# A long convolution split at half the sequence, and its kernel generated on one array tile per channel

## The chip, the cores and the metric

The program runs on one core of one Trainium2 chip. The metric is the device time of one execution in microseconds (us), median of several executions. A profile adds a span, which is the time from the first to the last instruction; it is about 1.9 us shorter than the timed execution. Engines are called PE (TensorE, the matrix engine), PEld (its weight loads, which overlap PE: in before the two are busy for 92% and 50% of the span), DVE (VectorE), ACT (ScalarE), POOL (GpSimd) and SP (SyncE, which issues most loads and stores). "N=256" is a matmul with 256 columns of moving data.

Every kernel below was timed alternately with the kernel before, on the same chip.

## The reference, cut to what matters

```python
def reference(u, A_re, A_im, B_re, B_im, C_re, C_im, log_dt, Dskip, x, w_gate, w_up, w_down):
    # L = 2048 positions, D = 512 channels, N = 128 modes per channel, F = 1792; x is u
    xn = layernorm(u)
    K  = einsum("dn,dnl,dn->dl", C, exp(dt * A * l), dt * B).real   # one kernel of 2048 taps per channel
    y  = irfft(rfft(pad(xn)) * rfft(pad(K)))[:L] + xn * Dskip       # causal convolution along the sequence
    g  = (sigmoid(xn @ w_gate) * (xn @ w_up)) @ w_down              # a gated linear unit (GLU)
    return u + y + g
```

The convolution and the GLU depend on `xn` alone, so they run interleaved: the GLU's matmuls fill TensorE while VectorE prepares the convolution.

## The kernel before

The convolution works in the frequency domain, with spectra of 4,096 points in 32 groups. The channels are in two column halves of 256 (`p`), and each half has 8 units (`u`) of four groups, so there are 16 units. The parts that matter:

```python
# 1. kernel generation: VectorE builds tables G and H for 128 channels, TensorE multiplies them.
#    Four channel blocks c, two halves each. G is one buffer: block c+1 seeds it after block c's matmuls.
for half_ in range(2):
    def f_k(...):
        for y in range(16 * half_, 16 * half_ + 16):
            R, h = 4 * (y % 4) + y // 8, y // 4 % 2
            pk = ...                                   # PSUM
            for comp in range(2):
                for t in range(2):                     # two column tiles of 64, two channels in each
                    r = slice(4 * R + 2 * t, 4 * R + 2 * t + 2)
                    T.matmul(pk[64 * t:64 * t + 64, y % 8, :], G[:, r, :, comp, h], H[:, r, :, comp, h],
                             start=(comp == 0), stop=(comp == 1), tile_position=(0, 64 * t))
# ...
# 2. one unit
def fm(...):  ...            # forward matmuls, 8 x N=256; evicted by ScalarE into xx, halves swapped by DMA
def fk(...):                 # spectrum of K: 20 matmuls of N=256 into a pair of PSUM banks
    for r in range(GB):      # GB = 4 groups
        for kt in range(NKT):          # NKT = 5
            T.matmul(two(sk)[:, DW * r:DW * r + DW], es()[:, r, kt, :], kT[p][:, kt, :], ...)
# ScalarE evicts it to kb, of which there is ONE slot
def fp(...):                 # the product of the spectra: one multiply of 128x2048 on VectorE
    V.tensor_tensor(out=pp()..., in0=xx()..., in1=kb().unsqueeze(1).to_broadcast([128, 2, GB * DW]), op=ALU.mult)
def fv(...):  ...            # product matmuls, 16 x N=256, into a PSUM pair; evicted, stored
```

A list `ORDER` fixes the order of all operations, so each engine has a fixed sequence. The change does not touch that list.

## Time and profile before

Time: 268.42 us median (267.21 to 268.91, 4 runs); the profiled execution, with a span of 262.9 us, is not one of these four, whose spans would be 265.3 to 267.0 us.

From about 20 to 145 us VectorE's row has only nines, and it is the first entry of the chain. From about 171 us on VectorE has holes, and TensorE carries the chain.

The groups of instructions of the parts that change (line, engine, operation, output and input, shape, count; then busy us and mean ns of one; then the engine's idle time before them and what ended it):

```profile
L817 DVE TENSOR_TENSOR big<-big 128x2048 bf16<-128x2048 bf16 x16 | 19.5, 1220 | 26.7 <-ACT big L813 15.6
L660 DVE TENSOR_TENSOR big<-big 128x256 bf16<-128x256 bf16 (+4 forms) x52 | 31.2, 600 | 2.8 <-ACT big L682 2.6
```

L817 is the product of the spectra, L660 the table work (its 2.6 us wait, at 149.9 us, is the one interruption of VectorE's chain; it waits for a block's tables to be released). TensorE's timeline gives the real cost of each group, from one start to the next (start, duration, operation, count; in brackets the idle time before it and what ended it):

```profile
82.50 2.12 PE L724 MATMUL pair_64<-big 128*64 128x42 bf16 x64
84.45 2.08 PE L724 MATMUL pair_63<-big 128*64 128x42 bf16 x64
...
145.15 0.63 PE L827 MATMUL pair_63<-big 64*64 64x256 bf16 x16 [0.70 <-ACT big L813]
...
158.70 2.35 PE L810 MATMUL pair_64<-big 128*128 128x256 bf16 x20
...
171.50 2.07 PE L724 MATMUL pair_63<-big 128*64 128x42 bf16 x62 [0.28 <-DVE big L666]
```

L724 is the kernel generation, L827 the product matmuls. A generation half takes 1.95 us (82.50 to 84.45), a K spectrum (L810) 2.18 us, and the last block's generation starts at 171.5 us. This last number is the yardstick: to its left VectorE sets the pace, to its right TensorE does.

### The profile page before, as it was taken

To read this page: it belongs to the slowest core of one execution; us is meant where nothing else is said; L and a number is where in the kernel's file an instruction comes from. 1 tells how busy PE (TensorE), PEld (TensorE's weight loads), DVE (VectorE), ACT (ScalarE), POOL (GpSimd) and SP (SyncE) were. 2 spreads that over 40 slices of the span, in tenths; PEclk is the share of its full clock that TensorE was granted. 3 is DMA by queue.
4 is the path that set the end of the run, shared out by engine and by line. 5 is a ranking of instruction groups with operands and counts; after the bars stand their busy time and mean duration, and the time that the engine had idled before them with its cause. 6 is when DMAs were issued, how large, how long until landed. Compare 5 with 4: busy or idle time off the path is not lost.

```text
span 262.9 us, 5705 instructions
## 1 busy us (share of the span) xinstructions
PE 243.0 (92%) x2254; PEld 131.4 (50%) x2254; DVE 192.9 (73%) x389; ACT 157.9 (60%) x247; POOL 21.7 (8%) x41
## 2 busy tenths in 40 slices
PE   7689998899999989989999999999999999999990
PEld 2353333334336444747567557477457656444440
DVE  3889999999999999999999599924111223566323
ACT  2699999999996544294674845752536776310000
POOL 1300220072000000102000000000020200000000
PEclk9999999999999999999999999999999999999997
DMA  7999975664559022857978846947997983496123
GB/s 163 161 295 323 339 220 145 190 139 107 145 202 157 15 80 80 228 178 143 306 216 253 228 118 193 271 124 235 302 306 175 308 261 96 131 264 201 44 67 100
DMA packets 50924, 49.34 MB, mean 188 GB/s; under 512 B 13137, under 2 KB 44114, under 8 KB 50770
## 3 DMA queue, kind: packets, MB, share of 16 engines
q1 hardware_dynamic: 47362, 44.66, 60.0%
q0 software_dynamic: 960, 1.57, 3.7%
q10 hardware_dynamic: 2576, 2.75, 3.6%
q8 instruction: 17, 0.28, 0.4%
q14 instruction: 9, 0.07, 0.1%
HBM read 30.36 MB, written 12.06 MB: 161 GB/s over the span
## 4 chain that ended last, share of the span: by engine, by line
DVE 47%; PE 28%; DMA 11%; SPq 4%; issue 3%; ACT 3%; DVEq 1%; POOL 1%; ACTq 0%
DVE big L661 8%; DVE big L660 8%; DVE hT_sb L928 8%; DVE big L665 5%; DVE big L666 5%; PE bank_68 L946 5%; SPq L382 4%; PE pair_64 L810 3%; DVE stats L482 3%; DMA big<-z_scr 3%; DMA big<-c_E 2%; DVE big L611 2%; PE bank_67 L921 2%; DMA big<-v_scr_94 2%; DVE big L609 2%
## 5 line engine op out<-in xcount | busy, mean ns | idle before, releaser
L946 PE MATMUL bank_68<-wd_sb,hT_sb 128*128 128x512 bf16 x196 | 44.7, 379 | 1.3 <-ACT glu_sb L976 1.1
L817 DVE TENSOR_TENSOR big<-big 128x2048 bf16<-128x2048 bf16 x16 | 19.5, 1220 | 26.7 <-ACT big L813 15.6
L906 PEld LDWEIGHTS <-wg_sb 128*128 128x128 bf16 x236 | 21.9, 97 | 29.1 <-issue 8.7
L921 PEld LDWEIGHTS <-wu_sb 128*128 128x128 bf16 x224 | 21.0, 97 | 28.8 <-issue 6.5
L946 PEld LDWEIGHTS <-hT_sb 128*128 128x128 bf16 x224 | 21.1, 98 | 27.6 <-issue 3.9
L810 PEld LDWEIGHTS <-big 128*128 128x128 bf16 x320 | 30.8, 98 | 6.7 <-DMA big<-c_E 1.4
L660 DVE TENSOR_TENSOR big<-big 128x256 bf16<-128x256 bf16 (+4 forms) x52 | 31.2, 600 | 2.8 <-ACT big L682 2.6
L661 DVE TENSOR_TENSOR big<-big 128x256 bf16<-128x256 bf16 (+4 forms) x52 | 31.3, 601 | 0.0
L921 PE MATMUL bank_67<-xnT,wu_sb 128*128 128x512 bf16 x88 | 22.6, 379 | 0.3 <-DVE hT_sb L928 0.2
L665 DVE TENSOR_TENSOR big<-big 128x128 bf16<-128x128 bf16 (+4 forms) x52 | 21.4, 412 | 0.6
L810 PE MATMUL pair_64<-big 128*128 128x256 bf16 x180 | 21.2, 273 | 0.6 <-DMA big<-c_E 0.6
L666 DVE TENSOR_TENSOR big<-big 128x128 bf16<-128x128 bf16 (+4 forms) x52 | 21.2, 407 | 0.0
L906 PE MATMUL bank_65<-xnT,wg_sb 128*128 128x512 bf16 (+1 forms) x80 | 19.7, 368 | 1.3 <-ACT hT_sb L915 0.9
L906 PE MATMUL bank_67<-xnT,wg_sb 128*128 128x512 bf16 (+1 forms) x76 | 18.5, 368 | 2.2 <-DVE hT_sb L928 2.2
L928 DVE TENSOR_TENSOR hT_sb<-hT_sb,bank_67 128x512 bf16<-128x512 bf16 x22 | 15.0, 682 | 7.4 <-PE bank_67 L921 7.3
L906 PE MATMUL bank_66<-xnT,wg_sb 128*128 128x512 bf16 (+1 forms) x80 | 19.7, 369 | 0.7 <-DVE hT_sb L928 0.4
L921 PE MATMUL bank_66<-xnT,wu_sb 128*128 128x512 bf16 x72 | 18.5, 380 | 0.2 <-ACT hT_sb L915 0.2
L921 PE MATMUL bank_65<-xnT,wu_sb 128*128 128x512 bf16 x64 | 16.4, 379 | 1.1 <-ACT hT_sb L915 0.5
L928 DVE TENSOR_TENSOR hT_sb<-hT_sb,bank_66 128x512 bf16<-128x512 bf16 x18 | 12.3, 681 | 6.7 <-PE bank_66 L921 3.8
L724 PEld LDWEIGHTS <-big 128*64 128x64 bf16 x512 | 16.1, 157 | 2.2 <-DVE big L666 1.0
L813 ACT ACTIVATE big<-pair_64 128x1024 bf16<-128x1024 f32 x9 | 9.2, 1023 | 13.3 <-PE pair_64 L810 11.1
L915 ACT ACTIVATE hT_sb<-bank_66 128x512 bf16<-128x512 f32 x19 | 11.7, 615 | 8.0 <-PE bank_66 L906 8.0
(117 smaller groups left out, 356.2 us busy)
## 6 DMA issues: line engine op xcount, KB each, us to landing
big<-c_E SPq DMA_DIRECT2D x16, 640.0 KB, 5.7
z_scr<-big SPq DMA_DIRECT2D x16, 256.0 KB, 2.8
big<-z_scr SPq DMA_DIRECT2D x16, 256.0 KB, 5.2
big<-big SPq DMA_DIRECT2D x64, 64.0 KB, 3.3
big<-in_A_u_dram SPq DMA_DIRECT2D x8, 256.0 KB, 7.5
v_scr_94<-big SPq DMA_DIRECT2D x8, 256.0 KB, 3.3
big<-v_scr_94 SPq DMA_DIRECT2D x8, 256.0 KB, 4.6
v_scr_95<-big SPq DMA_DIRECT2D x8, 256.0 KB, 4.0
```

The lines of the kernel that those rows point to most:

```text
L660: V.tensor_tensor(out=wide(outp), in0=lov, in1=mre, op=ALU.mult)
L661: V.tensor_tensor(out=wide(tb()), in0=lov, in1=mim, op=ALU.mult)
L665: V.tensor_tensor(out=outp[:, :, :, 0, :], in0=outp[:, :, :, 0, :], in1=tb()[:, :, :, 1, :], op=opr)
L666: V.tensor_tensor(out=outp[:, :, :, 1, :], in0=outp[:, :, :, 1, :], in1=tb()[:, :, :, 0, :], op=opi)
L724: T.matmul(pk[64 * t:64 * t + 64, y % 8, :], G[:, r, :, comp, h], H[:, r, :, comp, h], start=(comp == 0), stop=(comp == 1), tile_position= ...
L810: T.matmul(two(sk)[:, DW * r:DW * r + DW], es()[:, r, kt, :], kT[p][:, kt, :], start=kt == 0, stop=kt == NKT - 1)
L817: V.tensor_tensor(out=pp().rearrange("p c g d -> p c (g d)"), in0=xx().rearrange("p c g d -> p c (g d)"), in1=kb().unsqueeze(1).to_broadca ...
L906: T.matmul(bank(sl)[:, c0:c1], w[:, kt, k * 128:(k + 1) * 128], xnT[:, grp, kt, c0:c1], start=(kt == 0), stop=(kt == KT - 1))
L915: S.activation(out=hT_sb[:, hs.idx, k % 2, :], in_=bank(sl), func=ACT.Sigmoid)
L921: T.matmul(bank(sl), wu_sb[:, kt, k * 128:(k + 1) * 128], xnT[:, grp, kt, :], start=(kt == 0), stop=(kt == KT - 1))
L928: V.tensor_tensor(out=h(), in0=h(), in1=bank(sl), op=ALU.mult)
L946: T.matmul(bank(po), hT_sb[:, hts[k // 2].idx, k % 2, jj * 128:(jj + 1) * 128], wd_sb[:, k, :], start=(k == 0), stop=k == FT - 1, **kw)
```

## The change

The intent has two parts. **The split:** a causal convolution of 2,048 positions is done as three products of half-length blocks (first half of the input with both halves of K, second half of the input with the first half of K). The spectra then need 2,048 points, the K spectrum half as many matmuls and its table half the load; in exchange three half-size multiplies replace one. **The generation:** each channel gets an array tile of its own, 32 columns wide, four tiles side by side, so that no matmul computes products across channels that nobody uses.

The core of the diff (constants, forward matmuls, buffer places, prefix sums and the last-row correction cut):

```diff
             def f_k(half_=half_, sl=sl, G=G, H=H):
-                for y in range(16 * half_, 16 * half_ + 16):
-                    R, h = 4 * (y % 4) + y // 8, y // 4 % 2
-                    ...
+                for y in range(16):
+                    R, h = 16 * (y % 4) + 4 * (2 * half_ + y // 8), y // 4 % 2
                     for comp in range(2):
-                        for t in range(2):
-                            r = slice(4 * R + 2 * t, 4 * R + 2 * t + 2)
-                            T.matmul(pk[64 * t:64 * t + 64, y % 8, :], G[:, r, :, comp, h], H[:, r, :, comp, h], ...
+                        for t in range(4):
+                            T.matmul(pk[32 * t:32 * t + 32, y, :], G[:, R + t, :, comp, h], H[:, R + t, :, comp, h], ...
@@ one unit: spectrum of K
-                for r in range(GB):
+                for r in range(2):
                     for kt in range(NKT):
-                        T.matmul(two(sk)[:, DW * r:DW * r + DW], es()[:, r, kt, :], kT[p][:, kt, :], ...
+                        o = DW * (2 * r + kt // 4)
+                        T.matmul(two(sk)[:, o:o + DW], es()[:, r, kt, :], kT[p][:, kt, :], ...
@@ product
-                V.tensor_tensor(out=pp()..., in0=xx()..., in1=kb().unsqueeze(1).to_broadcast([128, 2, GB * DW]), op=ALU.mult)
+                xs = xx().rearrange("p c (r h) d -> p c r h d", h=2)
+                for q in range(2):
+                    V.tensor_tensor(out=pp()[:, q, :, 0:2, :], in0=xs[:, q],
+                                    in1=kb()[:, :, 0, :].unsqueeze(2).to_broadcast([128, 2, 2, DW]), op=ALU.mult)
+                V.tensor_tensor(out=pp()[:, :, :, 2, :], in0=xs[:, :, :, 0, :],
+                                in1=kb()[:, :, 1, :].unsqueeze(1).to_broadcast([128, 2, 2, DW]), op=ALU.mult)
@@ product matmuls
-                for a in range(0, GB, 2):                          # four rounds of N=256
+                for c0, c1, s0 in ((0, 2, True), (2, 3, False)):   # two rounds of N=512, two of N=256
```

## The prediction

> **What bounds the kernel now.** The chain of waits runs through VectorE from about 16 us to 143 us, and VectorE is over 97% busy in every 20 us stretch from 20 to 140. The list of VectorE's waits shows only one wait between 40 and 171 us (2.6 us at 149.9, for the kernel-generation matmuls to release a buffer). From 143 us on the chain is mostly TensorE, which idles under 2.5 us from 140 to 240. The gaps between groups in the timeline give TensorE's real cost per group: spectrum matmuls of K 2.18 us per unit of four groups (20 x N=256), product matmuls 0.56 us per unit, kernel generation 1.95 us per half (64 x N=42, two column tiles), four GLU matmuls 0.86 us. TensorE, VectorE and SyncE all run in a fixed order, which the change leaves as it is.
>
> **What changes, per unit (16 units).**
> - K spectrum: 10 matmuls instead of 20: TensorE -1.09 us.
> - Product matmuls: four rounds of N=256 become two of N=512 and two of N=256: about +0.21 us.
> - Forward matmuls: same columns, no change.
> - Product: one 128x2048 multiply (1.13 us from start to start) becomes three of 128x1024 (0.60 us each, as other multiplies of that size here, broadcast ones too): VectorE +0.67 us.
> - E load 640 to 320 KB.
>
> Kernel generation, 8 halves: 128 matmuls with 32-column weights instead of 64 with 64-column ones. [...] 48 on four 32-column tiles in about 0.5 us, 10 to 12 ns each. So I estimate 1.0 to 1.5 us per half, -0.65 us. The eviction (0.73 us) shrinks to about 0.45, off the path. Small VectorE additions: 0.3 us early, 1 us at 180, where VectorE idles.
>
> **How much is on the path.** Eight of the 16 products lie before 171.4 us, in VectorE's unbroken chain: +5.4 us, +0.3 us for the prefix sums, about -1.2 us because the 2.6 us wait shrinks. So the last VectorE work ahead of channel block 3's kernel generation comes about 4.5 us later. TensorE's savings before that (8 units, 7 us) buy nothing: it will wait for VectorE. The last kernel generation gives 1.3 us back, so TensorE is about 3 us late at 178. Eight units remain behind it: -8.7 + 1.7 = -7.0 us. But the transposed-spectrum loads that TensorE needs at 193.5 (it waits 0.3 us now) hang on an eviction at 171.3 and a queue of SyncE issues of 0.5 to 0.6 us each; they come about 2 us late even with less E traffic, and cost some 2 us. Sum: -2 us.
>
> **Predicted time: 266.0 us**, range 262.0 to 269.5. Faster by over 2%: 0.14; within 2%: 0.79; slower by over 2%: 0.07.
>
> **What would show it.** K-spectrum groups of about 1.09 us; products 3 x 0.60; kernel-generation halves at 1.0 to 1.5 us; new TensorE idle time of 3 to 7 us between 120 and 180, released by VectorE or by evictions that wait for it; the last kernel generation starting at about 176 instead of 171.5; a wait of about 2 us for the spectrum load near 195; the stretch from there to the end shorter by about 4 us.
>
> **What would make it wrong.** Four-way column tiles limited by issue or by strided weight reads: no gain or a loss in kernel generation (+2 to +4 us). Products slower than 0.60 us through the broadcast in the middle dimension. New waits in the tail because the fixed order was tuned to the old durations (+2 to +4 us), or none at the spectrum load (-2 us).

The 48 matmuls are selection matmuls in the trace of before (93.49 to 93.95 us from the first start to the last), and the estimate of 1.0 to 1.5 us per half rests on them alone. 5.4 + 0.3 - 1.2 = +4.5 us in front, of which the last generation gives 1.3 back (about +3), then -7.0 and +2 behind, together -2.

## More of the kernel before

PSUM holds two "pairs" (2 banks each) for all of the convolution, three banks for the GLU's first two matrices and one for its last.

TensorE is at full clock up to the last 4 us (the clock records have 0.50 from 259.03 us on).

The page of the profile. The first line is busy time of each engine and its share of the span. The rows of digits are 40 slices of the span, each digit the busy share in tenths, and PEclk is the clock granted to TensorE in tenths of full speed. The last line is the chain of waits that ended last, as shares of the span.

```profile
span 262.9 us, 5705 instructions
PE 243.0 (92%) x2254; PEld 131.4 (50%) x2254; DVE 192.9 (73%) x389; ACT 157.9 (60%) x247; POOL 21.7 (8%) x41
...
DVE  3889999999999999999999599924111223566323
...
PEclk9999999999999999999999999999999999999997
...
q8 instruction: 17, 0.28, 0.4%
...
DVE 47%; PE 28%; DMA 11%; SPq 4%; issue 3%; ACT 3%; DVEq 1%; POOL 1%; ACTq 0%
```

## The result, and the profile after

| | median us | lowest to highest | runs |
|---|---|---|---|
| before | 268.42 | 267.21 to 268.91 | 4 |
| after | 277.49 | 275.35 to 278.43 | 4 |

The ratio of the two is 1.0342, with a 95% interval of 1.0288 to 1.0396: 3.4% slower, and 8 us above the top of the predicted range. (All ratios here are the mean time of one kernel's fast runs over that of the other's of the same rounds, so not quite the ratio of the medians quoted.)

One caution for all that follows: the profiled execution of before (262.9 us) is shorter than every span recorded for this kernel in the later rounds (263.5 to 267.2 us). Differences between profiles therefore overstate a loss: after is 12.9 us longer by the profiles and 9.1 us by the medians.

The page of after, the same lines:

```profile
span 275.8 us, 6311 instructions
PE 232.2 (84%) x2519; PEld 112.7 (41%) x2546; DVE 205.9 (75%) x428; ACT 155.9 (57%) x247; POOL 21.8 (8%) x41
...
DVE  3899999999999799976999959990532545466313
...
PEclk9899999999997799959999789996899999999998
...
q8 instruction: 20, 0.33, 0.5%
...
PE 38%; DVE 31%; ACT 8%; issue 8%; DMA 7%; SPq 4%; DVEq 1%; POOL 0%; ACTq 0%
```

TensorE has 11 us less to do and is done 13 us later. Two new things show. VectorE's row of nines has gaps, and the chain now has 8% "issue" (3% before), time in which an engine waited for nothing that the profile shows. And the clock row has dips to between 5 and 8 in the middle of the run, four in all.

The groups (the product is now L829 and L831; L735 is the generation):

```profile
L829 DVE TENSOR_TENSOR big<-big 128x1024 bf16<-128x1024 bf16 x32 | 20.8, 685 | 16.2 <-ACT big L823 13.5
L672 DVE TENSOR_TENSOR big<-big 128x256 bf16<-128x256 bf16 (+4 forms) x52 | 31.2, 600 | 5.6 <-ACT big L694 5.2
```

The table wait that was 2.6 us is 5.2 us. TensorE's list of waits has long waits that it calls "issue" in one place only, the generation (L735; total, times and longest in us; 2.8 us more are in the other PSUM pair, and elsewhere none is over 0.3 us), and one long wait in the product matmuls (L841, 4.4 us):

```profile
PE pair_64 L735 <- issue: 7.2, 2, 5.1
```

In the timeline the generation looks like this (three of the four blocks; between them two K spectra, L821, 1.09 us from start to start; at the end the product matmuls that come between the halves of the remaining block):

```profile
82.73 1.37 PE L735 MATMUL pair_64<-big 128*32 128x21 bf16 x128
83.93 0.24 PE L735 MATMUL pair_63<-big 128*32 128x21 bf16 x8
86.97 1.19 PE L735 MATMUL pair_63<-big 128*32 128x21 bf16 x120 [2.80 <-issue]
...
111.43 1.22 PE L735 MATMUL pair_64<-big 128*32 128x21 bf16 x126
117.77 0.21 PE L735 MATMUL pair_64<-big 128*32 128x21 bf16 x2 [5.13 <-issue]
...
144.61 1.25 PE L821 MATMUL pair_64<-big 128*128 128x256 bf16 x10
145.70 1.26 PE L821 MATMUL pair_63<-big 128*128 128x256 bf16 x10
...
185.31 1.22 PE L735 MATMUL pair_63<-big 128*32 128x21 bf16 x124 [0.39 <-DVE big L678]
186.36 0.77 PE L735 MATMUL pair_64<-big 128*32 128x21 bf16 x55
189.23 0.80 PE L735 MATMUL pair_64<-big 128*32 128x21 bf16 x73 [2.10 <-issue]
...
155.24 1.50 PE L841 MATMUL pair_63<-big 64*64 64x512 bf16 x16 [4.44 <-ACT big L823]
```

A half that runs undisturbed takes 1.2 us, as predicted (82.73 to 83.93). But in three of four blocks the second half stops in the middle of a loop that waits for nothing, for 2.8, 5.1 and 2.1 us. What follows runs slowly: in slices of 1 us (busy time and count of PE, PEld, DVE, ACT, POOL, then clock, DMA share, GB/s) the granted clock falls just before TensorE starts again (86.21 and 86.97 us), and comes back at 93 us:

```profile
85.00:86.00 1.00, 0.00 (x0) 0.00 (x0) 0.97 (x4) 0.00 (x0) 0.00 (x0) 1.00 0.04 4
...
87.00:88.00 1.00, 1.00 (x120) 1.00 (x119) 1.00 (x3) 0.00 (x0) 0.00 (x0) 0.50 0.00 0
...
92.00:93.00 1.00, 1.00 (x4) 0.36 (x3) 1.00 (x3) 0.49 (x2) 0.00 (x0) 0.50 0.00 0
```

The clock records of the trace give four such stretches, each of 6.83 us at half clock: from 86.21, 116.93, 154.47 and 188.61 us, one at each of the four waits above (and one of 3.41 us at 11.11 us, while the input is still being loaded). Before had none until its last 4 us. A wait by itself does not decide it. The four stretches start 30.72, 37.54 and 34.14 us apart, which is 9, 11 and 10 times 3.41 us, half the length of a stretch, and the short one starts 22 times 3.41 us ahead of the first. So whether a wait costs the clock may depend on when it comes; no run tests this, but the wait of 2.80 us in block 0 has such a stretch, and one of 2.93 us at the same place of gen_only (run 2, from 84.56 us) has none. Of the four pieces of 3.41 us just ahead of the drops, two hold no matmul at all (inside the waits of 5.1 and 4.4 us). The other two hold 1.4 and 1.8 us of generation matmuls beside the waits of 2.8 and 2.1 us, while a piece of the same trace with 1.9 us of large matmuls (168.13 to 171.54 us) cost no clock. That the small matmuls of the generation count for little is my guess from this: 1.8 and 1.9 us are close, and before ran 3.97 us of its own generation matmuls at full clock (82.50 to 86.47 us). Run 6 has a stronger case of it, but no run tests it alone.

With the yardstick, the span splits into two parts (the start of the last block's generation proper, from the timeline; the rest of the span after it):

| profiled run of | first generation starts | last generation starts | from there to the end | span |
|---|---|---|---|---|
| before | 82.5 | 171.5 | 91.4 | 262.9 |
| after | 82.7 | 185.3 | 90.5 | 275.8 |
| split_only (run 1) | 82.3 | 178.7 | 87.4 | 266.1 |
| gen_only (run 2) | 83.1 | 177.4 | 93.0 | 270.4 |
| split_mul1 (run 6) | 83.8 | 175.0 | 87.5 | 262.6 |
| split_order (run 7) | 83.1 | 175.4 | 88.8 | 264.3 |
| hybrid2 (run 13) | 83.4 | 174.6 | 87.8 | 262.4 |

By the profiles all 12.9 us are lost in the first part (13.8 us later at the yardstick), and the part where TensorE carries the chain gives back only 0.9 us. The first column shows how far two executions can be apart before any generation has run, up to 1.5 us (split_only and split_mul1), so differences of that size in the second column mean nothing.

### Where the generation stops: a count of instructions

The stops come in the middle of a loop, so I counted what TensorE had executed when each came, and set beside it the records of the instruction queue. Its loads are of 16,384 bytes each. I took such a block for 256 instructions, and the counts fit: at the three stops of after TensorE had begun 479, 991 and 1,885 weight loads, so with one matmul to each the stops are 1,024 and 1,788 instructions apart, 4.00 and 6.98 times 256. With one matmul to each weight load of the page TensorE's program has 4,508 instructions before and 5,092 after, 17.6 and 19.9 times 256, and the page shows 17 and 20 loads. A generation half after the change, 128 matmuls and as many weight loads, is exactly one block, and lasts 1.1 us; before it was half a block, and 256 instructions lasted 3.9 us.

All three stops lie at the same place of a block. In the five rows below TensorE does not execute past the point 0.73 of a block (counted from the first instruction in the trace) before the fetch that started behind the previous such point has landed. This table is worked out from the records of the trace (us; good to a few tenths where matmul records are sparse):

```
                      passes the point   fetch starts   lands     next point        margin
before, block 0            82.64            84.67       85.83     87.34 reached      +1.5
before, block 3           173.24           173.56      175.00    177.22 reached      +2.2
after,  block 0            82.79            84.64       85.58     stood from 84.17, went on at 86.97
after,  block 1           111.40           115.55      116.51     stood from 112.65, went on at 117.77
after,  block 3           185.77           186.59      187.88     stood from 187.13, went on at 189.23
```

From passing the point to landing took 2.1 to 5.1 us after the change (1.8 to 3.2 in the two rows of before), and another 1.3 to 1.4 us went by until TensorE executed again. Before, 256 instructions of generation lasted 3.9 us, and of the two rows of before the tighter has 1.5 us to spare; after, they last 1.1 us. In the worst case (block 1) the fetch started 4.2 us after the point was passed; the DMA engines were full then (share 1.02 to 1.13 from 110 to 114 us), but whether this delayed it was not tested.

### The profile page after: what moved, and what is told of

The parts are those of the page before. It is cut to its first block, busy times and chain, and to the rows that moved or that the text cites. A ratio compares the mean times of both kernels' runs of the same rounds, so it can differ in the third digit from the quotient of the medians.

```text
span 275.8 us, 6311 instructions
## 1 busy us (share of the span) xinstructions
PE 232.2 (84%) x2519; PEld 112.7 (41%) x2546; DVE 205.9 (75%) x428; ACT 155.9 (57%) x247; POOL 21.8 (8%) x41
## 4 chain that ended last, share of the span: by engine, by line
PE 38%; DVE 31%; ACT 8%; issue 8%; DMA 7%; SPq 4%; DVEq 1%; POOL 0%; ACTq 0%
PE bank_68 L965 10%; DVE hT_sb L947 6%; DVE big L673 5%; DVE big L672 5%; SPq L392 4%; DVE big L829 3%; PE bank_66 L940 3%; PE bank_65 L940 3%; PE bank_67 L940 3%; DVE big L678 3%; DMA big<-c_E 2%; PE bank_67 L925 2%; DVE big L677 2%; ACT hT_sb L934 2%; PE bank_65 L925 2%
## 5 line engine op out<-in xcount | busy, mean ns | idle before, releaser
L965 PE MATMUL bank_68<-wd_sb,hT_sb 128*128 128x512 bf16 x189 | 46.4, 395 | 2.0 <-ACT glu_sb L995 1.1
L965 PEld LDWEIGHTS <-hT_sb 128*128 128x128 bf16 x224 | 21.8, 101 | 29.8 <-issue 7.4
L940 PEld LDWEIGHTS <-wu_sb 128*128 128x128 bf16 x224 | 21.6, 100 | 29.8 <-issue 8.6
L829 DVE TENSOR_TENSOR big<-big 128x1024 bf16<-128x1024 bf16 x32 | 20.8, 685 | 16.2 <-ACT big L823 13.5
L940 PE MATMUL bank_67<-xnT,wu_sb 128*128 128x512 bf16 x83 | 22.7, 388 | 0.5 <-issue 0.2
L925 PE MATMUL bank_66<-xnT,wg_sb 128*128 128x512 bf16 (+1 forms) x79 | 20.1, 378 | 2.3 <-DVE hT_sb L947 1.5
L925 PE MATMUL bank_67<-xnT,wg_sb 128*128 128x512 bf16 (+1 forms) x72 | 19.5, 391 | 2.3 <-DVE hT_sb L947 1.5
L925 PE MATMUL bank_65<-xnT,wg_sb 128*128 128x512 bf16 (+1 forms) x75 | 18.9, 368 | 0.7 <-issue 0.2
L940 PE MATMUL bank_66<-xnT,wu_sb 128*128 128x512 bf16 x69 | 18.8, 393 | 0.8 <-ACT hT_sb L934 0.4
L841 PE MATMUL pair_63<-big 64*64 64x256 bf16 (+1 forms) x176 | 11.8, 350 | 8.6 <-ACT big L823 4.4
L823 ACT ACTIVATE big<-pair_64 128x1024 bf16<-128x1024 f32 x9 | 9.2, 1024 | 15.9 <-DVE big L831 11.4
L940 PE MATMUL bank_65<-xnT,wu_sb 128*128 128x512 bf16 x62 | 17.2, 396 | 0.8 <-ACT hT_sb L934 0.6
L821 PEld LDWEIGHTS <-big 128*128 128x128 bf16 x160 | 15.3, 98 | 5.2 <-issue 2.4
L841 PEld LDWEIGHTS <-big 64*64 64x64 bf16 x256 | 7.3, 111 | 20.2 <-issue 13.5
```

The costliest lines, as they stand in the source:

```text
L821: T.matmul(two(sk)[:, o:o + DW], es()[:, r, kt, :], kT[p][:, kt, :], start=kt % 4 == 0, stop=kt >= 3)
L829: V.tensor_tensor(out=pp()[:, q, :, 0:2, :], in0=xs[:, q], in1=kb()[:, :, 0, :].unsqueeze(2).to_broadcast([128, 2, 2, DW]), op=ALU.mult)
L841: T.matmul(two(sv)[h ^ x:(h ^ x) + 64, 512 * r + 256 * (not s0):512 * r + 512], mab[h:h + 64, 2 * u + r, q, :], pp()[h:h + 64, q, r, c0:c1 ...
L925: T.matmul(bank(sl)[:, c0:c1], w[:, kt, k * 128:(k + 1) * 128], xnT[:, grp, kt, c0:c1], start=(kt == 0), stop=(kt == KT - 1))
L940: T.matmul(bank(sl), wu_sb[:, kt, k * 128:(k + 1) * 128], xnT[:, grp, kt, :], start=(kt == 0), stop=(kt == KT - 1))
L965: T.matmul(bank(po), hT_sb[:, hts[k // 2].idx, k % 2, jj * 128:(jj + 1) * 128], wd_sb[:, k, :], start=(k == 0), stop=k == FT - 1, **kw)
```

## The experiments

Two theories were to be tested, each with its rival.

- **The generation.** Theory: the multiplications are as fast as predicted, and the stops are the instruction fetch; the half clock doubles their cost. Rival: the array or the memory reads of 32-column tiles stall (the prediction's own doubt, "limited by issue or by strided weight reads").
- **The split.** Theory: it loses through VectorE's extra 0.67 us per unit in the unbroken chain. Rival: the price is in TensorE's waits, and the clock after them.

Runs 1 to 4 were made together, 5 to 8 and 9 to 11 likewise, 12 and 13 alone. The kernel before took 266.11 us (7 runs), 265.94 (7), 266.38 (7), 266.95 (11) and 266.17 (11) in these rounds.

### Run 1, split_only: the split with the generation of before

```diff
@@ after, generation
-                for y in range(16):
-                    ...for t in range(4): ... tile_position=(0, 32 * t)
+                for y in range(16 * half_, 16 * half_ + 16):
+                    ...for t in range(2): ... tile_position=(0, 64 * t)      # as before
```

> The changed kernel with the kernel generation of before (64-column tiles, 128 matmuls per channel block instead of 256). Theory F (instruction fetch: 256 TensorE instructions in 1.1 us outrun the fetch of the next 16 KB of instructions, TensorE stands for 2 to 5 us, and its clock is then halved for 6.8 us): no idle time put down to issue above 0.5 us inside the generation, granted clock above 0.985, 17 to 18 instruction fetches of 16 KB, and about 263 to 267 us, since the convolution split alone should do what the prediction said. Rival S (the split itself costs: 0.67 us more VectorE time per unit, 8 units on the path, plus a fixed order tuned to other durations): still slower than before, 272 us or more.

Measured: 269.69 us (268.02 to 270.96, 4 runs), ratio 1.0144 (1.0106 to 1.0182). No stop with "issue" is left in the generation, and the whole-run clock is 0.979 in the profiled run, 0.966 to 0.969 in the others (above 0.985 was expected). The time lies between the two expectations, so neither theory has it whole. The single costs are as predicted: K spectrum 1.10 us, products 1.21 + 0.60 us. But TensorE has a wait of nearly 4 us between the generation's first half of block 2 (L736) and the product matmuls, and the latter run at half clock:

```profile
141.67 2.11 PE L736 MATMUL pair<-big 128*64 128x42 bf16 x64
147.72 1.49 PE L843 MATMUL pair<-big 64*64 64x512 bf16 x16 [3.94 <-ACT big L825]
```

What it waits for is seen on VectorE and ScalarE:

```profile
144.65 1.30 DVE L831 TENSOR_TENSOR big<-big 128x1024 bf16<-128x1024 bf16 x2
145.86 0.70 DVE L833 TENSOR_TENSOR big<-big 128x1024 bf16<-128x1024 bf16 x1
...
146.65 1.02 ACT L825 ACTIVATE big<-pair 128x1024 bf16<-128x1024 f32 x1 [4.27 <-DVE big L833]
```

The product of one unit (L831, L833) comes late because VectorE is behind. It holds the one `kb` slot, so ScalarE can't evict the next unit's K spectrum until 146.65, so the PSUM pair is not free for the product matmuls until 147.7. These stand in TensorE's fixed order before the second generation half of block 2. This half then ends late, and VectorE waits 4.5 us for the release of the tables (2.6 before). The circle is closed: VectorE is late, makes TensorE late, and then waits for TensorE. Then 6.83 us of half clock from 145.89 make it later.

What follows: the split alone costs 1.4%, about 40% of the loss. The prediction's own terms without the gain of the generation make it about -0.7 us.

### Run 2, gen_only: the generation on four column tiles, in the kernel before

```diff
@@ before, generation: the f_k, f_e and kq edits of the change, nothing else
-                        for t in range(2): ... tile_position=(0, 64 * t)
+                        for t in range(4): ... tile_position=(0, 32 * t)
```

> The kernel before with only the kernel generation changed to 32-column tiles. Theory F: stalls of 2 us or more put down to issue in two or more of the four channel blocks, windows of half clock after them, mean granted clock 0.95 to 0.97, slower than before by 3 to 8 us (271 to 277 us). Rival S: no slower than before, perhaps 1 to 3 us faster (265 to 268 us), because the generation itself takes 1.1 us per half instead of 1.95.

Measured: 274.70 us (272.35 to 279.67, 4 runs of which one, 279.67, is slow and left out of the ratio), ratio 1.0287 (1.0232 to 1.0342). The stops are there without any split, in all four blocks (2.9, 4.6, 1.2 and 2.1 us). Two of them cost the clock (6.83 us from 113.33, 3.41 us from 181.60); the 2.9 us of block 0 did not. The stop of block 1:

```profile
109.30 2.31 PE L723 MATMUL pair<-big 128*32 128x21 bf16 x254
116.21 0.21 PE L723 MATMUL pair<-big 128*32 128x21 bf16 x2 [4.60 <-issue]
```

254 matmuls in a row took 2.3 us, 9 ns each with their weight loads, before the stop. So neither array nor reads are slow.

What follows: the generation alone costs 2.9%. In the table above the two parts nearly add up at the yardstick: 7.2 us later with the split, 5.9 us with the generation, 13.8 us with both. By the times they don't: 1.4% and 2.9% are more than the 3.4% of both, by 0.9 points, about as much as the intervals allow.

### Run 3, shift30: the same program, 60 instructions further along

If the stops come from fetched blocks, they are tied to the count of instructions and not to the code. 30 tiny matmuls (60 instructions with their weight loads) in front of the whole program must move each stop by a number known in advance.

```diff
@@ after
-    keep_warm(14, -10)
+    # 30 matmuls of one column (and their weight loads) ahead of the same 14 warm-up matmuls
+    for _ in range(30):
+        T.matmul(bank(wsl)[0:32, 0:1], glu_sb[:, 0, 0:32], glu_sb[:, 0, 0:1], start=True, stop=True, tile_position=(0, 0))
+    keep_warm(14, -10)
```

> The changed kernel with 30 tiny weight-load and matmul pairs (60 instructions) more at the very start of TensorE, nothing else. Theory F: a stall falls where TensorE needs the next block of 256 instructions, so it moves 30 pairs earlier within the generation: from after 8 matmuls of block 0's second half to about 106 matmuls (a whole page later, since the page now begins in the middle of the first half), block 1 from 126 to about 96, block 3 from 55 to about 25; sizes 2 to 5 us as before, time 275 to 279 us. Rival T (the tiles themselves or their PSUM writes stall[...]): stalls stay at the same matmuls.

Measured (one look, so of unknown state): 277.46 us. The stops went exactly where they were expected:

```profile
84.65 2.29 PE L742 MATMUL pair<-big 128*32 128x21 bf16 x234
89.66 0.38 PE L742 MATMUL pair<-big 128*32 128x21 bf16 x22 [2.71 <-issue]
109.84 2.36 PE L742 MATMUL pair<-big 128*32 128x21 bf16 x224
116.17 0.45 PE L742 MATMUL pair<-big 128*32 128x21 bf16 x32 [3.96 <-issue]
...
187.98 1.14 PE L742 MATMUL pair<-big 128*32 128x21 bf16 x103 [2.54 <-issue]
```

Block 0 stops after 234 matmuls (136 in after), block 1 after 224 (254 in after), block 3 after 153 (183 in after). In blocks 1 and 3 that is 30 matmuls earlier. In block 0 the points where a fetch is needed lay at 8 and 136 matmuls, and the next would have been at 264; 30 earlier the first falls ahead of the generation and the others lie at 106 and 234, so that the fetch which is started at 106 is missed at 234. Nothing that the array or the reads do knows these numbers. This settles where the stops come from; what they and the half clock are worth in time it does not say.

### Run 4, apart: other matmuls between the two halves

```diff
@@ shift30, ORDER: GLU groups moved between the two generation halves of blocks 0, 1 and 3
-    ..., 258, 253, 224, 223, ...
+    ..., 258, 253, 685, 687, 686, 723, 224, 223, ...
-    ..., 295, 306, 267, 266, ...
+    ..., 295, 306, 749, 267, 266, ...
-    ..., 572, 576, 353, 574, ...
+    ..., 572, 576, 771, 772, 841, 353, 574, ...
```

> The 30 pairs of shift30, and GLU matmuls moved between the two halves of the generation in block 0 (12 matmuls), block 1 (14) and block 3 (8), so that a block of 256 instructions takes about 3 to 4 us instead of 1.1. Theory F: stalls put down to issue shrink to under 1.5 us each, at most one window of half clock is left, granted clock 0.975 or more, and about 6 to 11 us faster than the changed kernel (266 to 271 us), with the same instruction count. Rival T: clock and time as in the changed kernel (275 us or more).

Measured: 274.10 us (272.71 to 277.52, the last slow and left out), ratio 1.0277 (1.0217 to 1.0336). The stops shrink from 9.2 us in sum (in shift30) to two of 1.3 and 1.4 us, as there is more time for the fetch: in block 0 the second half starts 3.98 us after the first (84.99 and 88.97 us), 1.20 us in after.

```profile
117.14 0.57 PE L706 MATMUL pair<-big 128*32 128x21 bf16 x46 [1.32 <-issue]
```

What follows: the cure works on the stops and is worth less than I expected (266 to 271 us). Against 1.0342 for after the intervals overlap, so a gain in time is not shown at all. The half clock came all the same, from 119.67 us and, after the split's wait, which is 4.8 us long here, from 150.39 us.

### Run 5, split_warm: dummy matmuls against the half clock, in the pair that is waited for

The rival for the split: is the price of its 3.9 us wait the idle clock? Useless matmuls during the wait should keep the clock up.

```diff
@@ split_only, ahead of the product matmuls of unit 5, first column half
+                if p == 0 and u == 5:
+                    for _ in range(14):
+                        T.matmul(two(sv)[:, 0:512], wg_sb[:, 0, 0:128], xnT[:, 0, 0, :], start=True, stop=True, ...)
```

> split_only with 14 unused matmuls of N=512 (3.0 us) put into the 3.9 us in which TensorE waits at 144 us for the product of unit 5; same results, same order. Theory H (the wait itself is one cost, the half clock that follows it for 6.8 us is a second one): no half-clock window near 146 us, granted clock 0.99 or more, the second half of block 2's generation starts about 2 us earlier than 152.4, and the whole is 1.5 to 3 us faster than split_only. Rival W (only the wait counts, the clock falls into idle time anyway): no faster than split_only, within 0.5 us.

Measured: 272.27 us (271.23 to 273.74, 4 runs), ratio 1.0220 (1.0167 to 1.0273). A miss, and a mistake of mine: the dummies write to the PSUM pair that is waited for, so they waited 3.96 us themselves and ran after it, instead of during it. The run says only that the wait is for the PSUM pair, since nothing else could hold these dummies.

### Run 6, split_mul1: one multiply instead of three (wrong result)

```diff
@@ split_only, product
-                for q in range(2): ... 128x1024
-                V.tensor_tensor(... 128x1024)
+                V.tensor_tensor(out=pp()[:, :, :, 0:2, :]..., in0=xx()..., in1=kb()....to_broadcast([128, 2, 2, 2 * DW]), op=ALU.mult)
@@ product matmuls: the third block reads the first block's place
-                for c0, c1, s0 in ((0, 2, True), (2, 3, False)):
+                for c0, c1, s0 in ((0, 2, True), (0, 1, False)):
```

> split_only with one product multiply of 128x2048 instead of three of 128x1024 (wrong result on purpose: the third block product is replaced by the first), so VectorE pays 1.13 us per unit as in the kernel before; all TensorE work, loads and evictions of the split stay. Theory V (VectorE's extra 0.67 us per unit, 8 of them ahead of block 3's generation, is what eats the split's gain): the wait of 3.9 us at 144 shrinks to under 2 us, no half clock there, block 3's generation starts 5 to 7 us earlier than 178.7, and the time is 5 to 9 us below split_only, that is 3 us or more faster than before. Rival (loads, eviction order or the TensorE order itself eat it): less than 3 us below split_only.

Measured: 264.42 us (262.97 to 265.36, 4 runs), ratio 0.9914 (0.9853 to 0.9975), with a relative error of 0.038 as intended. Everything else of the split is unchanged: the ratio is 2.3% below that of split_only, some 6 us (3.5 us by the two profiled runs). The yardstick comes 3.6 us earlier, and the part behind it takes the same time (87.5 and 87.4 us). So the two more multiplies cost in front of the yardstick, where VectorE has no idle time, and nothing behind it, where it has. The expected gain over the kernel before was at least 3 us, and only 2.3 us came. Two other points were missed: TensorE's wait shrank to 2.8 us and not under 2, and the half clock behind it stayed (6.83 us from 144.38), so this gain is not one of the clock. The clock halved once more, at 178.52 us, and with no wait ahead of it: for 3.35 of the 3.41 us before, TensorE was busy with these matmuls of block 3's generation:

```profile
175.04 4.29 PE L736 MATMUL pair<-big 128*64 128x42 bf16 x128
```

### Runs 7 and 8, split_order and before_order: two products earlier in VectorE's order

```diff
@@ ORDER, same three moves in split_only and in the kernel before: products of the last units ahead of table work of block 3
-    ..., 435, 424, 439, 367, 340, 422, 343, 344, 341, ...
+    ..., 435, 424, 439, 440, 425, 367, 340, 422, 343, 344, 426, 341, ...
```

> split_only with two product multiplies (units 5 and 4) moved ahead of block 3's table multiplies in VectorE's order, about 4 us and 1 us earlier, and the eviction of the K spectrum between them moved along; no work added or removed. Theory V and H: TensorE's wait at 144 us under 1.5 us, no half clock there, VectorE's wait for block 2's generation 4.5 us shrinks to 1 to 2.5 us, block 3's generation starts 3 to 5 us earlier, 3 to 5 us faster than split_only, that is level with the kernel before or up to 2 us faster. Rival: the delay only moves to block 3's table, within 1 us of split_only.

> The same move in the kernel before, as a control: it waits only 0.7 us for this product, so at most 2 us faster and more likely within 1 us. If it gains as much as split_order does, the move is an improvement of its own and says nothing about the split.

Measured: split_order 266.81 us (266.20 to 268.68, 4 runs), ratio 1.0023 (0.9969 to 1.0076); the control before_order 267.31 us (267.11 to 267.56, 4 runs), ratio 1.0030 (0.9991 to 1.0070). VectorE's wait for the tables falls from 4.5 to 0.5 us. TensorE's wait halves and comes at another place, ahead of the generation's first half, with no half clock behind it (a short one, of 3.41 us, comes at 178 us):

```profile
144.59 2.11 PE L700 MATMUL pair<-big 128*64 128x42 bf16 x64 [1.95 <-ACT big L789]
```

What follows: of the 1.4% of the split, 1.2 points were the place of two products in the order, which was made for the kernel before with its shorter ones; the same moves bring the kernel before nothing.

### Run 9, split_warm2: the dummies again, in a bank that is free

```diff
@@ split_only, ahead of the product matmuls of unit 5, first column half
+                for _ in range(16 if warm else 0):      # warm: the free bank of the GLU's last matrix
+                    T.matmul(bank(warm), wg_sb[:, 0, 0:128], xnT[:, 0, 0, :], start=True, stop=True)
```

> split_only with 16 unused matmuls of N=512 (3.5 us) ahead of the product matmuls of unit 5, written to the free bank of the down projection this time: split_warm's went to the bank pair that TensorE was itself waiting for, so they ran after the wait and not in it. Theory H (the half clock after the wait is a cost of its own): no half-clock window near 146 us, block 2's second half starts 1.5 to 2.5 us earlier than in split_only, time 1 to 3 us below split_only (ratio to before about 1.005). Rival W: ratio to before within 0.3% of split_only's 1.0144.

Measured: 267.76 us (266.59 to 269.08, 4 runs), ratio 1.0035 (0.9982 to 1.0088). Work that nobody needs makes the kernel about 1.1 points faster than split_only, 2.9 us (1.2 to 4.6 by the two intervals):

```profile
144.53 3.63 PE L842 MATMUL bank<-xnT,wg_sb 128*128 128x512 bf16 x16
148.49 0.84 PE L847 MATMUL pair<-big 64*64 64x512 bf16 x16 [0.34 <-ACT big L825]
```

L842 are the dummies. The product matmuls behind them take 0.84 us instead of 1.49, and the clock records have no half clock near 146 us. The wait itself is still there; only its clock is saved. The second half of block 2 starts at 151.01 us instead of 152.39. So the rival was right too: by these means about three quarters of the split's 1.4% are the half clock after a single wait. Runs 6, 7 and 9 (2.3, 1.2 and 1.1 points) all work on the same lateness, so their gains overlap and can't be added.

### Run 10, split_order2: a GLU group against the half clock at 178 us

```diff
@@ split_order, ORDER: one GLU group between the halves of block 3's generation
-    ..., 572, 576, 353, 574, ...
+    ..., 572, 576, 771, 353, 574, ...
```

> split_order with one GLU group (4 matmuls of N=512) moved between the two halves of block 3's generation, so that TensorE's 4 us of small matmuls there do not end in a window of half clock (178.0 to 181.4 in split_order's trace). If that window costs, 0.5 to 1.5 us below split_order and at most level with the kernel before (ratio 0.997 to 1.001); if not, level with split_order (1.0023).

Measured: 267.75 us (266.31 to 268.94, 4 runs), ratio 1.0048 (0.9992 to 1.0104): no gain over split_order, though the stretch of half clock at 178 us is gone from its trace. A miss, and a warning that not every such stretch costs time that can be seen.

### Run 11, split_pool: the third multiply on GpSimd

```diff
@@ split_order, product
-                V.tensor_tensor(out=pp()[:, :, :, 2, :], ...)
+                P.tensor_tensor(out=pp()[:, :, :, 2, :], ...)
```

> split_order with the third multiply of each product (128x1024) given to GpSimd, which is idle for 92% of the span. If it takes no more than 2 us there and leaves VectorE's speed alone, VectorE is freed of 0.60 us per unit and the time falls by 2 to 5 us below split_order, below both kernels (ratio to before about 0.985 to 0.995). If GpSimd and VectorE get in each other's way [...], multiplies on GpSimd take 3 us or more or VectorE's own get longer, and it is slower than split_order.

Measured: 285.44 us (284.40 to 288.40, 4 runs), ratio 1.0714 (1.0640 to 1.0788). The groups of the products:

```profile
L797 POOL TENSOR_TENSOR big<-big 128x1024 bf16<-128x1024 bf16 x16 | 44.7, 2793 | 65.0 <-DMA big<-big 37.6 <-ACT big L789 27.3
L795 DVE TENSOR_TENSOR big<-big 128x1024 bf16<-128x1024 bf16 x32 | 41.3, 1327 | 20.9 <-ACT big L789 19.7 <-DMA big<-big 1.0
```

GpSimd takes 2.79 us where VectorE takes 0.68 (4.1 times), and VectorE's own multiplies take 1.33 us on average instead of 0.69 (1.9 times) now that GpSimd works beside it; by what it holds them up the run does not show. Taking work off the bottleneck engine made that engine slower: its 32 remaining multiplies are busy for 41.3 us, and the same 32 in after for 20.8.

### Runs 12 and 13, hybrid and hybrid2: the split for the second column half alone

The table of the yardstick says where the split can pay: behind it. There all 8 units of the second column half lie, and VectorE has idle time. This kernel uses the old form for the first half, the split for the second, and the old generation.

```diff
@@ before, one unit (the new functions are those of the change)
+            fm = fm1 if p else fm          # likewise fk, fp, fv; both sets of constants are loaded
@@ hybrid: the split form's product matrices (512 KB) go out behind the table load of unit 0, second half
+            le = dma("SP", es, ..., after=ld_mabn if p == 1 and u == 0 else None)
@@ hybrid2: the same load goes out earlier, behind the first load of the transposed spectrum
+            lds.append(dma("SP", vps[p][t], ..., after=ld_mabn if p == 0 and t == 0 else None))
```

> The split at half the sequence for the second column half alone (8 of the 16 units, the ones that run after 178 us, where VectorE has idle time); the first column half and the whole kernel generation as in the kernel before. If the loss of the split comes from VectorE's unbroken chain before 171 us and the wait it makes there, this kernel has none of it up to 178 us: the last generation's first half starts within 1 us of the 171.5 us of the kernel before, there is no wait of TensorE over 3 us and no half clock between 120 and 180 us. After that TensorE saves 8 x 0.87 = 7.0 us, of which the split alone showed about 4 to reach the end (its last generation ended 7.2 us later, its span was 3.2 us longer). Expected 262 us, range 260 to 264.5, that is 1 to 2% faster than the kernel before. Rival: the second half is not bound by TensorE as a whole but by loads and evictions, or the three short multiplies cost there too: then 265 to 268, no difference.

Measured: 270.68 us (268.74 to 272.00, 6 runs), ratio 1.0137 (1.0094 to 1.0179). A miss, from a fault of the experiment. The load that only this kernel has landed late, TensorE waited 6.2 us for it, and the clock was at 0.83 over 180 to 200 us:

```profile
PE pair L999 <- DMA big<-c_MABn: 6.2, 1, 6.2
```

That load was moved, and the run repeated:

> As the run before (the split for the second column half alone), with one load moved: the product matrices of the split form (512 KB) went out as the last of a row of loads at 187.3 us and TensorE waited 6.2 us for them, then ran at half clock; here they go out behind the first load of the transposed spectrum, at about 178.5 us, as early as VectorE's tables leave their place free. If that wait was all that spoilt it, no TensorE wait over 2 us is left between 120 and 240 us, the clock over the whole run is at least 0.98, and the 6.2 us and half of 6.8 us come off 270.7: 261 us, range 259.5 to 264, faster than the kernel before by 1 to 2.5%. If the split's cheaper spectrum brings nothing even where VectorE has idle time (the second half bound by loads and evictions), 265 or more.

Measured: 264.24 us (263.00 to 265.61, 6 runs) against 266.17 (11 runs), ratio 0.9917 (0.9867 to 0.9968). This is the one correct kernel that is faster than the kernel before: by 0.8%, with the interval below 1, though under the 2% that the prediction counted as a change. It lies just above the range expected (259.5 to 264), and the gain is just under the 1 to 2.5% expected.

Of the saving behind the yardstick this gives a clean measurement, by one profiled execution of each. The stretch from the last generation's start to the last GLU matmuls, in two pieces, in before and then in hybrid2 (columns as above); the piece after it takes 23.9 us in both:

```profile
171.50:206.00 34.50, 34.18 (x438) 22.48 (x442) 7.48 (x13) 16.62 (x22) 1.63 (x2) 1.00 0.82 238
206.00:239.00 33.00, 32.67 (x276) 17.75 (x264) 15.77 (x20) 16.94 (x23) 1.64 (x2) 1.00 0.71 204
```

```profile
174.64:206.10 31.46, 29.49 (x364) 17.47 (x372) 11.07 (x25) 17.03 (x22) 1.63 (x2) 1.00 0.77 226
206.10:238.50 32.40, 30.83 (x242) 15.23 (x234) 18.24 (x28) 16.91 (x23) 1.64 (x2) 1.00 0.69 193
```

With the last piece (17.6 and 17.5 us busy) TensorE's busy time falls by 6.6 us, from 84.5 to 77.9, close to the 7.0 us predicted. The stretch falls by 3.6 us (91.4 to 87.8). The other 3.0 us turn into idle time of TensorE (6.9 to 9.9 us): in the pieces shown it has nothing to do for 3.5 us, where before it had 0.7. The list of waits spreads this over loads of spectra, multiplies and evictions, none over 0.9 us.

hybrid2 still reaches the yardstick 3.1 us later than the profiled before, 0.9 us of it already at the first generation, with a wait of 1.3 us for a load at 151.5 us and a stretch of 3.41 us at half clock beginning there. Why that load was late was not traced; it stays open, and with it some 2 us that such a kernel might still gain.

## Why the prediction was wrong, point by point

**What held.** VectorE's chain to 171 us bounds the kernel before. The single costs were right: K spectrum 1.10 us (predicted 1.09), products 1.81 us per unit from start to start (1.80), product matmuls 0.77 us (0.56 + 0.21), generation halves of 1.1 to 1.25 us while they run (1.0 to 1.5). The estimate for four column tiles held: 128 matmuls and as many weight loads took 1.1 us, 9 ns for each pair (run 2), against 30 ns for each of the 64 pairs of a half before (1.95 us).

**The failed step for the generation.** "So I estimate 1.0 to 1.5 us per half, -0.65 us" stopped at the array. It costed instructions by what they do and not by the supply of instructions. Eight halves of 256 instructions at 1.1 us each ran into a fetch that took 2.1 to 5.1 us in after (that this is what stops them: runs 2 and 3). In the place of "-0.65 us" per half stand stops of 2.8, 5.1 and 2.1 us in three blocks and 6.83 us of half clock behind each. By itself, with the stops of run 2, the generation is +2.9%, the larger part of the loss; how this divides into stops and half clock is not shown (run 4 took most of the stops away without a clear gain). The prediction did list "limited by issue" as a danger, at "+2 to +4 us"; alone it measured 7.6 us by the ratio.

**The failed step for the split, first part.** "About -1.2 us because the 2.6 us wait shrinks": it grew, to 4.5 us in the split alone. The slower VectorE delays, by way of the one `kb` slot and the PSUM pair, TensorE's fixed order, and this delays the release for which VectorE waits (run 1). And "it will wait for VectorE" was taken as free: TensorE's savings "buy nothing", but the wait costs nothing either. In fact TensorE lost its clock after it: 6.83 us at half speed, worth 2.9 us of time (1.2 to 4.6, run 9). Instead of +4.5 us the yardstick moved by +7.2 us.

**The failed step for the split, second part.** "-8.7 + 1.7 = -7.0 us" behind the yardstick, less "some 2 us" for the transposed-spectrum loads. TensorE's work did fall by 6.6 us there. The predicted single wait of 2 us near 195 us did not come (0.3 us in after); small waits of 3.0 us in sum did, so -3.6 us arrived (run 13). In after only -0.9 us arrived; that the generation's last stop and its half clock ate the rest is likely (gen_only is 1.6 us longer behind the yardstick than before) but was not tested.

**The sum.** Predicted: +4.5 in front, of which the generation gives 1.3 back, -5 behind, about -2. Measured by the profiles: +13.8 in front (7.2 split, 5.9 generation, 0.7 of the two together), -0.9 behind, +12.9 (+9.1 by the times). The sign was wrong because two terms were missing that do not appear in any duration of the kernel before: the instruction supply and the clock that TensorE loses.

**What stays open:** why the fetch of block 1 started 4.2 us after the point was passed; how much of the generation's loss is the half clock, and whether its small matmuls alone can bring it on, and what decides whether a wait does; and what makes the wait at 151.5 us in hybrid2.

## What to carry to other kernels

Count instructions as well as columns: when a change cuts work into more and smaller matmuls, compare the time that 256 of TensorE's instructions take (1.1 us here) with the time that a fetch takes (2 to 5 us here), and look in the trace for waits with "issue" in the middle of a loop. Charge an idle TensorE for its clock, not only for the wait (here 6.83 us at half clock after a wait of 3.94 us, run 1; and look at the clock records of stretches with small matmuls only: 3.35 us of them lost it without any wait in run 6), and if the wait can't be removed, matmuls into a free bank through it can pay (2.9 us here). And give the cheaper-on-one-engine form only to the stretch in which that engine is the limit: the same split that cost 1.4% everywhere gained 0.8% in the second half alone.
